# Attention and channel mix: q, k and v loaded as rows of two tokens, pair order kept through attention and mixing, and the masks of two units added by the matrix engine

## The chip, the cores and the metric

The kernel runs on one core of a Trainium2 chip. The metric is the time of one execution on the device in microseconds (us). The executions of the kernel before lay within about two per cent of each other on each chip, so each comparison uses several executions of both kernels on the same chip. An execution over 1.5 per cent above the fastest of its kernel in its round counts as slow. That is one each of four_sinks, before_bias_mix, one_sink_less_both and before_less_pe, and one or two of the kernel before in three of the five rounds. The medians and ranges quoted include them; the ratios do not, and every profiled execution is a fast one.

Names in the profile: PE is the matrix engine (PEld its weight loads), DVE the vector engine, ACT the scalar engine, POOL GpSimd, SP the engine that issues most loads and stores. A name with q behind it (SPq) is that engine's sequencer at work, for instance issuing a load.

## The reference

Attention with a sliding window of 128 tokens and four sink tokens that every query may see, then a channel mix (two layers with a squared relu between them, and a sigmoid gate), in fp32:

```python
B, H, S, D = 4, 8, 768, 64
keep = (pos_k < 4) | ((pos_q - pos_k >= 0) & (pos_q - pos_k < 128))
a = softmax(where(keep, q @ k.T / 8, -1e9)); x = (a @ v) as [B, S, 512]
x_prev = x shifted by one token, zeros first
xk = mu_k * x + (1 - mu_k) * x_prev      # mu_k, mu_r: one factor per channel
xr = mu_r * x + (1 - mu_r) * x_prev
out = sigmoid(xr @ w_r) * (relu(xk @ w_k) ** 2 @ w_v)     # w_k 512x1024, w_v 1024x512
```

## The kernel before

The work is cut into 12 units of 256 tokens, three to each of the four sequences. The order of instructions on each engine is a fixed list, made beforehand and written in the kernel, and a small model of the engines decides how the lists are interleaved and where filler matmuls go. The parts that the change and the argument touch (cuts marked):

```python
# k of units 0 to 3, q of units 0 to 7: one 512-byte row of two tokens per packet;
# v, and the other k and q: one token, 256 bytes
nc.sync.dma_start(out=buf[key][:, h0:h1, :, :]..., in_=src[b, h0:h1, ...].rearrange(
    "h (p j) d -> p h (j d)", j=2))
nc.sync.dma_start(out=buf[key][:, g, :, :],                  # v, g = 0, 1
    in_=v[b, :, s0:s0 + 128, :].rearrange("h p d -> p h d"))
...
# the values of the four sink tokens, spread over partitions by a matmul with 0/1 weights
nc.tensor.matmul(out=buf[psk]..., lhsT=spread, rhs=buf["vb", u][:, 0, :, 0:D], ...)
nc.vector.tensor_tensor(out=vsink[b % 2][:, :, 0:D], in0=buf[psk]..., in1=hmask..., op=ALU.mult)
...
# masks: after the exponential, on the vector engine, in every unit
nc.vector.tensor_tensor(out=at, in0=at, in1=m, op=ALU.mult)
...
# mix: one operation per 128 channels, t0 - 1 is the token before
nc.vector.scalar_tensor_tensor(out=buf[key][:, c0 + i, :], in0=buf[tk][:, i, :],
    scalar=mu[w][:, c0 + i:c0 + i + 1], in1=xt[:, c0 + i, t0 - 1:t0 + 255],
    op0=ALU.mult, op1=ALU.add)
```

Loads are issued by SP in the order of its list. In the built program they take turns on eight semaphores, and a load waits for the one eight places earlier to have landed before it is issued.

The softmax here doesn't subtract the row's maximum and nothing guards it: scores larger than these inputs give would overflow.

Of the kernel before, what the change touches and what calls it, by code (L numbers as in the profile page):

```python
# [16 lines left out]

CHOICE = {
    78: "ACT", 81: "ACT", 82: "ACT", 84: "ACT", 86: "ACT", 88: "DVE", 93: "DVE", 94: "DVE", 96:
    "DVE", 100: "DVE", 101: "DVE", 127: "DVE", 133: "DVE", 135: "DVE", 136: "DVE", 139: "ACT",  # L20
    140: "DVE", 149: "DVE", 190: "DVE", 191: "ACT", 192: "ACT", 217: "DVE", 264: "DVE", 272:
    "DVE", 277: "DVE", 304: "DVE", 342: "DVE", 345: "DVE", 347: "DVE", 351: "ACT", 353: "DVE",
    360: "DVE", 422: "DVE", 428: "ACT", 429: "ACT", 498: "DVE", 500: "DVE", 503: "DVE", 506:
    "DVE", 507: "ACT", 519: "DVE", 585: "ACT", 586: "ACT", 653: "DVE", 657: "DVE", 659: "DVE",
    662: "DVE", 671: "DVE", 735: "DVE", 737: "ACT", 738: "DVE", 743: "DVE", 750: "DVE", 814:
    "DVE", 815: "ACT", 824: "DVE", 884: "DVE", 886: "DVE", 890: "ACT", 891: "ACT", 1002: "DVE",
# [5 lines left out]
XD = ()  # L32
# [16 lines left out]
        89, 92, 105, 95, 98, 103, 116, 108, 113, 131, 137, 141, 128, 124, 119, 155, 134, 157,  # L49
        148, 183, 189, 168, 235, 207, 208, 211, 212, 219, 220, 160, 165, 171, 176, 215, 193,  # L50
        180, 200, 216, 186, 237, 290, 298, 291, 294, 299, 302, 248, 303, 225, 295, 240, 245,
        306, 223, 227, 276, 231, 228, 251, 260, 232, 266, 256, 310, 263, 283, 269, 311, 318,
        343, 308, 314, 329, 315, 348, 366, 374, 367, 375, 321, 370, 394, 326, 371, 332, 337,
        396, 274, 352, 378, 359, 379, 382, 407, 384, 386, 421, 387, 444, 452, 445, 453, 399,
        426, 404, 474, 410, 415, 390, 430, 391, 456, 437, 457, 448, 472, 485, 449, 462, 525,
        529, 526, 530, 499, 537, 460, 504, 538, 468, 509, 469, 553, 477, 482, 533, 493, 488,
        534, 511, 564, 556, 464, 578, 465, 541, 518, 543, 561, 549, 583, 572, 550, 587, 545,
        567, 631, 601, 546, 602, 605, 613, 606, 594, 629, 642, 614, 619, 609, 617, 610, 639,
        634, 677, 681, 678, 682, 663, 645, 689, 705, 707, 685, 650, 686, 690, 625, 670, 718,
        710, 621, 626, 693, 622, 760, 756, 764, 757, 761, 765, 721, 695, 740, 726, 715, 774,  # L60
        784, 701, 749, 768, 742, 769, 795, 702, 787, 792, 697, 772, 698, 816, 776, 780, 777,
        781, 834, 830, 838, 831, 835, 798, 839, 858, 860, 842, 803, 846, 843, 823, 854, 848,
        868, 863, 871, 855, 906, 914, 907, 850, 915, 851, 879, 874, 910, 892, 911, 918, 899,
        919, 934, 936, 922, 924, 930, 947, 931, 972, 939, 973, 980, 944, 981, 950, 976, 958,
        977, 955, 984, 926, 965, 985, 927, 990, 988, 1000, 1008, 1004, 1001, 1012, 1005, 1013,
        1009, 992, 1020, 996, 993, 997, 1016, 1018, 1021, 1028, 1024, 1029, 1025,
    ),
    "DVE": (
        70, 71, 88, 93, 94, 100, 96, 107, 101, 112, 109, 114, 110, 136, 104, 115, 118, 127, 123,
        143, 125, 120, 133, 121, 126, 135, 149, 144, 150, 151, 145, 152, 190, 146, 159, 147,  # L70
        164, 79, 80, 153, 69, 170, 140, 175, 161, 162, 166, 172, 167, 177, 173, 178, 154, 195,
        196, 202, 197, 204, 203, 210, 217, 198, 222, 205, 206, 83, 239, 244, 304, 199, 85, 241,
        305, 242, 246, 214, 247, 255, 218, 87, 277, 250, 293, 297, 278, 229, 252, 301, 253, 233,
        257, 258, 279, 264, 342, 285, 347, 280, 281, 286, 288, 345, 320, 287, 312, 325, 316,
        272, 336, 289, 322, 331, 323, 327, 282, 328, 333, 338, 334, 339, 369, 353, 275, 373,
        354, 360, 357, 361, 381, 355, 377, 363, 356, 362, 422, 388, 398, 403, 409, 400, 414,
        405, 401, 365, 411, 416, 406, 417, 412, 358, 364, 447, 432, 392, 433, 439, 434, 441,
        440, 455, 459, 498, 481, 476, 503, 451, 528, 500, 487, 506, 435, 492, 510, 436, 470,
        478, 479, 483, 443, 484, 494, 555, 495, 489, 540, 490, 442, 536, 557, 571, 513, 558,
        560, 532, 466, 514, 519, 562, 520, 563, 516, 566, 573, 521, 574, 515, 522, 589, 551,  # L80
        568, 590, 569, 517, 524, 547, 523, 653, 633, 592, 638, 596, 659, 598, 657, 591, 597,
        604, 644, 635, 640, 636, 641, 649, 599, 616, 600, 612, 665, 646, 593, 608, 647, 651,
        709, 652, 668, 662, 666, 692, 667, 711, 671, 672, 674, 673, 675, 712, 627, 680, 623,
        669, 735, 720, 714, 725, 722, 723, 676, 684, 727, 728, 688, 759, 716, 741, 717, 763,
        791, 786, 750, 767, 738, 743, 788, 789, 793, 744, 703, 794, 745, 771, 751, 747, 802,
        746, 753, 752, 754, 699, 818, 778, 782, 797, 819, 748, 821, 833, 799, 755, 800, 837,
        804, 805, 814, 862, 841, 867, 824, 825, 820, 845, 826, 864, 827, 865, 869, 884, 856,
        822, 878, 886, 870, 828, 873, 852, 875, 880, 881, 876, 909, 829, 917, 894, 897, 913,
        901, 895, 921, 902, 938, 903, 943, 896, 932, 949, 940, 941, 945, 946, 951, 954, 952,
        904, 956, 957, 898, 960, 961, 905, 967, 975, 962, 969, 968, 928, 979, 963, 971, 987,  # L90
        983, 1002, 964, 1003, 1007, 970, 1011, 1015, 994, 998, 1022, 1030, 1026,
    ),
    "ACT": (
        91, 90, 97, 111, 106, 99, 68, 67, 117, 130, 122, 132, 142, 138, 129, 182, 188, 163, 158,
        184, 78, 156, 174, 169, 81, 139, 209, 221, 236, 213, 179, 185, 194, 201, 181, 191, 187,
        243, 238, 292, 82, 300, 192, 254, 226, 249, 84, 296, 307, 86, 224, 259, 265, 261, 262,
        268, 267, 284, 270, 340, 324, 319, 344, 309, 335, 330, 349, 368, 376, 395, 372, 418,
        402, 397, 380, 420, 383, 423, 408, 385, 413, 351, 425, 446, 454, 427, 480, 475, 431,
        496, 438, 428, 501, 458, 450, 473, 486, 463, 527, 531, 429, 491, 461, 505, 539, 559,
        554, 507, 577, 535, 512, 570, 575, 579, 580, 582, 542, 544, 565, 584, 585, 588, 637,  # L100
        632, 603, 586, 655, 595, 607, 615, 630, 620, 643, 618, 611, 648, 679, 683, 664, 706,
        708, 713, 687, 691, 731, 729, 719, 733, 694, 724, 737, 758, 766, 762, 696, 775, 790,
        785, 770, 808, 796, 806, 801, 773, 812, 810, 817, 832, 836, 840, 859, 861, 866, 844,
        847, 815, 882, 849, 877, 872, 888, 908, 916, 893, 912, 900, 935, 920, 937, 942, 890,
        923, 891, 925, 948, 974, 953, 982, 959, 966, 986, 978, 991, 989, 1006, 1014, 1010, 1019,
        1017,
    ),
    "POOL": (
        73, 72, 74, 75, 76, 102, 77, 273, 271, 350, 508, 661, 739,
    ),  # L110
    "SP": (
        0, 1, 2, 3, 4, 5, 7, 6, 16, 8, 9, 10, 11, 15, 17, 12, 18, 13, 14, 19, 20, 25, 23, 24,
        21, 234, 22, 341, 346, 28, 30, 29, 313, 26, 27, 419, 424, 31, 230, 33, 34, 35, 32, 497,
        36, 317, 502, 37, 40, 38, 389, 39, 45, 393, 41, 576, 581, 42, 467, 43, 44, 46, 47, 654,
        656, 660, 658, 548, 48, 51, 49, 50, 471, 53, 52, 732, 730, 734, 736, 54, 628, 57, 58,
        55, 552, 56, 624, 809, 807, 704, 813, 811, 59, 60, 61, 779, 63, 64, 62, 700, 883, 885,
        889, 887, 65, 857, 66, 853, 933, 929, 783, 995, 999, 1023, 1031, 1027,
    ),
}


class Plan:







# [151 lines left out]
def kernel(  # L281
# [19 lines left out]
    NS = 4  # L301
# [15 lines left out]
    pool("bank", 8 - 2 * TOGETHER, [128, 512], FP32, psum)  # L317
    for name in ("ks", "qs", "vs"):
        pool(name, 3, [128, 2, H, D] if name == "vs" else [128, H, 2, D], FP32)
    pool("w32", 3, [128, NC, 512], FP32)  # L320
    pool("kb", 3, [128, 2, H, D], BF16)
    pool("qb", 3, [128, 2, H, D], BF16)
    pool("kt", 4, [128, NP, 2, 128], BF16)
    pool("qt", 4, [128, NP, 2, 128], BF16)
    pool("e", 5, [128, 2, 512], BF16)
    pool("es", 3, [128, 256], BF16)
    pool("rec", 6, [128, 2, 2, 1], FP32)
    pool("x", 3, [128, 2, Dm], BF16)
    pool("td", 3, [128, 2, 256], BF16)
# [630 lines left out]
```

## Time and profile before

The time before is 172.48 us, the median of 3 runs (171.81 to 172.6).

| what | before |
|---|---|
| span of the profiled execution | 169.6 us |
| PE / DVE / ACT busy | 94% / 90% / 76% |
| first matmul with wk / with wv | 21.75 us / 39.30 us |
| last matmul starts | 166.15 us |
| PE's gaps after 40 us | 3.0 us |
| v of unit 3 is issued | 40.8 us |

The first two rows are on the page; the rest is read from single instructions in the trace. For "PE's gaps" I take the starts of consecutive matmuls and subtract what a matmul of its size costs when PE is full; what is over by more than 60 ns is summed. A stretch at half clock counts as gaps too. The lines of the profile itself are in the prediction.

### The profile page before, as it was taken

What the parts mean: (1) busy time and instruction counts of PE and PEld (TensorE: products, weight loads), DVE (VectorE), ACT (ScalarE), POOL (GpSimd) and SP (SyncE); (2) the same over time, 40 slices, a digit from 0 to 9 for tenths busy, and PEclk for the clock granted to TensorE, in tenths of its full rate; (3) what the DMA queues carried; (4) which work ended last, traced back from release to release, by engine and by line L of the source; (5) the groups of instructions that cost most, each with busy time, mean ns of one, the idle gap of its engine ahead of it and who ended that gap; (6) DMA issues with size and microseconds to landing.
All of it is one profiled execution on the core that took longest, in us unless ns stands there. A gap on an engine that the chain in (4) does not pass through costs nothing.

```text
span 169.6 us, 4184 instructions
## 1 busy us (share of the span) xinstructions
PE 160.0 (94%) x1602; PEld 105.7 (62%) x1602; DVE 153.4 (90%) x403; ACT 129.0 (76%) x208; POOL 13.5 (8%) x31
## 2 busy tenths in 40 slices
PE   7977879799999999999999999999999999999992
PEld 2544658664657667767567786756476775877551
DVE  6288898999999999999999999999999999799542
ACT  3588797999898999897979986866829849953320
POOL 6330000000200010050000200030000000000000
PEclk9995699999999999999999999999999999999999
DMA  5999989999938979999579489969969858103033
GB/s 142 238 275 320 344 192 326 356 335 276 191 86 214 254 172 231 184 263 287 135 183 221 97 207 225 181 168 233 252 147 266 195 109 233 62 4 124 2 124 124
DMA packets 82803, 33.82 MB, mean 199 GB/s; under 512 B 64736, under 2 KB 77280, under 8 KB 82784
## 3 DMA queue, kind: packets, MB, share of 16 engines
q1 hardware_dynamic: 81728, 33.56, 80.0%
q8 instruction: 12, 0.20, 0.5%
q10 hardware_dynamic: 1056, 0.00, 0.4%
q14 instruction: 7, 0.06, 0.1%
HBM read 24.12 MB, written 6.29 MB: 179 GB/s over the span
## 4 chain that ended last, share of the span: by engine, by line
PE 82%; DVE 10%; DMA 3%; SPq 1%; issue 1%; ACT 0%; POOL 0%; DVEq 0%
PE bank L888 24%; PE bank L839 23%; PE bank L870 12%; PE bank L713 7%; PE sc L654 6%; DMA vs<-in_v_dram 3%; PE bank L752 3%; PE bank L569 2%; PE bank L701 2%; DVE e L690 2%; DVE xk L789 2%; SPq L387 1%; DVE x L729 1%; PE bank L631 1%; PE bank L809 1%
## 5 line engine op out<-in xcount | busy, mean ns | idle before, releaser
L839 PE MATMUL bank<-xk,wk_sb 128*128 128x256 bf16 x384 | 50.5, 273 | 1.1 <-DVE wk_sb L513 0.9
L676 ACT ACTIVATE e<-sc 128x1024 bf16<-128x1024 f32 (+1 forms) x48 | 44.6, 966 | 4.4 <-PE sc L654 4.4
L888 PE MATMUL bank<-wv_h,kk 128*128 128x512 bf16 x184 | 45.8, 379 | 0.0
L839 PEld LDWEIGHTS <-wk_sb 128*128 128x128 bf16 x384 | 35.3, 98 | 9.3 <-DVE wk_sb L513 1.4
L849 ACT ACTIVATE rl<-bank 128x512 bf16<-128x512 f32 x45 | 26.2, 607 | 10.3 <-PE bank L839 7.8
L690 DVE TENSOR_TENSOR e<-e,mask 128x1024 bf16<-128x1024 bf16 (+1 forms) x48 | 30.1, 639 | 0.4 <-POOL ksink L608 0.3
L888 PEld LDWEIGHTS <-kk 128*128 128x128 bf16 x184 | 16.7, 98 | 15.7 <-issue 0.5
L870 PE MATMUL bank<-wr_sb,xr 128*128 128x512 bf16 x96 | 24.2, 379 | 0.0
L789 DVE SCALAR_TENSOR_TENSOR xk<-td,mu,xt 128x256 bf16<-128x256 bf16 x48 | 22.4, 493 | 0.1
L789 DVE SCALAR_TENSOR_TENSOR xr<-td,mu,xt 128x256 bf16<-128x256 bf16 x48 | 22.5, 477 | 0.0
L876 ACT ACTIVATE th<-bank 128x512 f32<-128x512 f32 x24 | 14.8, 620 | 7.8 <-PE bank L870 7.7
L729 DVE TENSOR_TENSOR x<-bank,rec 128x256 bf16<-128x256 f32 x48 | 19.4, 416 | 0.6 <-DVE rec L726 0.3
L897 DVE SCALAR_TENSOR_TENSOR ob<-th,bank 128x512 f32<-128x512 f32 x23 | 15.6, 681 | 4.7 <-ACT th L876 2.6
L861 DVE TENSOR_TENSOR kk<-rl 128x512 bf16<-128x512 bf16 x48 | 19.4, 416 | 0.1
L713 PE MATMUL bank<-vb,e 128*128 128x65 bf16 x352 | 19.2, 195 | 0.2
L713 PEld LDWEIGHTS <-e 128*128 128x128 bf16 x352 | 16.7, 99 | 3.1 <-issue 0.6
L654 PE MATMUL sc<-qt,kt 64*128 64x128 bf16 (+1 forms) x256 | 14.8, 247 | 1.1 <-ACT kt L577 0.7
L870 PEld LDWEIGHTS <-xr 128*128 128x128 bf16 x96 | 8.9, 98 | 8.6 <-issue 0.3
L654 PEld LDWEIGHTS <-kt 64*128 64x128 bf16 x256 | 9.5, 97 | 7.3 <-issue 4.0
L761 ACT COPY xt<-bank 128x512 bf16<-128x512 bf16 x15 | 8.8, 587 | 5.3 <-PE bank L752 4.5
L701 PE MATMUL bank<-vsink,es 128*128 128x130 bf16 x64 | 12.4, 220 | 0.3 <-ACT rl L849 0.3
L779 DVE TENSOR_TENSOR td<-xt 128x512 bf16<-128x512 bf16 x24 | 10.5, 440 | 0.1
(63 smaller groups left out, 163.9 us busy)
## 6 DMA issues: line engine op xcount, KB each, us to landing
vs<-in_v_dram SPq DMA_DIRECT2D x24, 256.0 KB, 4.6
out_dram<-ob SPq DMA_DIRECT2D x23, 256.0 KB, 3.3
ks<-in_k_dram SPq DMA_DIRECT2D x18, 256.0 KB, 4.8
qs<-in_q_dram SPq DMA_DIRECT2D x7, 512.0 KB, 7.3
qs<-in_q_dram SPq DMA_DIRECT2D x10, 256.0 KB, 5.3
w<-in_moe_w_k_dram SPq DMA_DIRECT2D x2, 1024.0 KB, 10.3
w<-in_moe_w_v_dram SPq DMA_DIRECT2D x2, 1024.0 KB, 10.0
ks<-in_k_dram SPq DMA_DIRECT2D x3, 512.0 KB, 8.2
```

What stands on the lines that cost most here:

```text
L654: nc.tensor.matmul(out=sc[:, a, o0:o1], lhsT=lhs[rows], rhs=rhs[rows], start=True, stop=True)
L676: nc.scalar.activation(out=buf[ek][:, :, lo:], in_=buf[sck][:, :, lo:], func=AF.Exp, scale=scale)
L690: nc.vector.tensor_tensor(out=at, in0=at, in1=m, op=ALU.mult)
L701: nc.tensor.matmul(out=o[:, g, :, :], lhsT=buf["es", u][:, 128 * g:128 * g + 128], rhs=vsink[b % 2][:, 2 * c:2 * c + 2, :], start=True, st ...
L713: nc.tensor.matmul(out=o[:, g, a, :], lhsT=e[:, a, e0:e0 + 128], rhs=rhs, start=(T == 0 and i == 0), stop=(i == len(blocks) - 1), skip_gro ...
L729: P.op("DVE", dve(256), lambda ok=ok, rk=rk, c=c: nc.vector.tensor_tensor(out=buf["x", u][:, :, 128 * c:128 * c + 128].rearrange("p g (a d ...
L789: nc.vector.scalar_tensor_tensor(out=buf[key][:, c0 + i, :], in0=buf[tk][:, i, :], scalar=mu[w][:, c0 + i:c0 + i + 1], in1=xt[:, c0 + i, t ...
L839: nc.tensor.matmul(out=ps[:, i, :], lhsT=wk_sb[:, c, 128 * f:128 * f + 128], rhs=xk[:, c, :], start=(c == 0), stop=(c == NC - 1), skip_gro ...
L849: nc.scalar.activation(out=buf[rk], in_=buf[psk].rearrange("p (i t) -> p i t", i=2), func=AF.Relu)
L861: P.op("DVE", dve(512, 0.52), lambda f2=f2, rk=rk: nc.vector.tensor_tensor(out=buf["kk", u][:, 2 * f2:2 * f2 + 2, :], in0=buf[rk], in1=buf ...
L870: nc.tensor.matmul(out=buf[psk], lhsT=buf["xr", u][:, c, 128 * g:128 * g + 128], rhs=wr_sb[:, c, :], start=(c == 0), stop=(c == NC - 1))
L888: nc.tensor.matmul(out=buf[psk], rhs=wv_h[:, f, :], lhsT=buf["kk", u][:, f, 128 * g:128 * g + 128], start=(f == 0), stop=(f == NF - 1))
```

## The change

Its intent: fewer and larger packets in the load of v; no de-interleaving of q and k any more, because scores, values and mixing all work in pair order; less work for DVE in the opening, where PE waits for attention; and a mix that uses cheaper DVE operations. The core of the diff, cut:

```diff
+BIAS = (0, 1)                                    # units masked by the matrix engine
-  in_=v[b, :, s0:s0 + 128, :].rearrange("h p d -> p h d")      # two loads per unit
+  all of q, k, v: "h (p j) d -> p h (j d)", j=2    # one load per unit (units 0 to 2: two)
...
+# values of the half unit behind, moved to the other 64 partitions (16 copies)
+copy(out=buf[vj][64 - 64 * g:128 - 64 * g]..., in_=buf["vb", w][64 * g:64 * g + 64]...)
...
-  nc.tensor.matmul(out=buf[psk]..., lhsT=spread, rhs=buf["vb", u][:, 0, :, 0:D], ...)
+  def sink_rows():                               # once for each of four sequences
+      for h in range(H):
+          at = 32 * (h // 2) + 4 * (h % 2)
+          nc.sync.dma_start(out=vs32[b % 2][at:at + NS, :], in_=v[b, h, 0:NS, :])
...
+  nc.tensor.matmul(out=buf["sc", u, c][:, a, :], lhsT=ident, start=True,     # u in BIAS
+                   rhs=bias[T].to_broadcast([128, 2, 2, 128]), stop=False, ...)
...
-  nc.vector.scalar_tensor_tensor(...)            # 96 times
+  nc.vector.tensor_scalar(out=buf[key][:, c0 + i, :], in0=buf[tk][:, i, :],  # 96 times
+      scalar1=mu[w][:, c0 + i:c0 + i + 1], scalar2=None, op0=ALU.mult)
+  nc.vector.tensor_tensor(out=at, in0=at, in1=behind(c0), op=ALU.add)        # 48 times
-P.fill_until = 22000.0
+P.fill_until = 32000.0
```

The lists of order were made anew for all engines. Among other things the loads of wk now come later in the queue.

## The prediction

> **What bounds the kernel now.** I read the page first: busy shares, slices, chain. Then the windows of busy time, to find when the matrix engine becomes full, then the chain of waits in order of time, for what one matmul costs when it is full, and last the DMA issues with their landings.
>
> ```profile
> span 169.6 us, 4184 instructions
> PE 160.0 (94%) x1602; PEld 105.7 (62%) x1602; DVE 153.4 (90%) x403; ACT 129.0 (76%) x208; POOL 13.5 (8%) x31
> PE   7977879799999999999999999999999999999992
> PEclk9995699999999999999999999999999999999999
> DMA  5999989999938979999579489969969858103033
> PE 82%; DVE 10%; DMA 3%; SPq 1%; issue 1%; ACT 0%; POOL 0%; DVEq 0%
> ```
> ```profile
> 15.00:20.00 5.00, 4.64 (x53) 3.28 (x52) 3.73 (x12) 3.92 (x7) 0.00 (x0) 0.50 1.05 378
> 20.00:25.00 5.00, 3.24 (x29) 2.16 (x26) 5.00 (x12) 5.00 (x8) 0.00 (x0) 0.98 0.89 199
> ...
> 35.00:40.00 5.00, 5.00 (x44) 2.97 (x43) 5.00 (x14) 5.00 (x9) 0.00 (x0) 1.00 1.16 310
> 40.00:50.00 10.00, 10.00 (x97) 5.63 (x96) 9.96 (x26) 9.38 (x17) 1.25 (x3) 1.00 0.85 180
> ...
> 120.00:140.00 20.00, 20.00 (x201) 13.69 (x200) 19.80 (x52) 13.66 (x23) 0.00 (x0) 1.00 0.85 190
> ```
> ```profile
> 40.55 1.73 PE bank L888 x8
> ...
> 57.75 0.55 PE sc L654 x12
> ...
> 90.46 1.75 PE bank L839 x16
> ```
> In the slices the matrix engine (PE) is full from the ninth slice (about 34 us) to the end, and the chain, 82% PE, stays on it. Before that it has holes, and near 15 to 20 us runs at half clock. The windows (columns: stretch, length, busy PE, weight load, DVE, ACT, POOL, clock, DMA share, GB/s) say that from 20 us DVE and ACT are full too, and DMA is saturated until 40 us. The chain gives the price of a full PE: 109 ns for a 256-column matmul, 216 ns for 512, and 0.55 us for a pair of score tiles.
>
> With these prices and the spacings of matmul starts in the trace I add up what PE must do: 384 first-layer matmuls x 0.109 = 41.9 us; 184 second-layer x 0.216 = 39.7 and 16 half ones 1.7; 96 gate x 0.216 = 20.7; score pairs 16 x 0.548 + 8 x 0.436 = 12.3; 352 value matmuls x 0.029 = 10.2; 192 transposes x 0.056 = 10.8; sink work 3.6 + 0.9; the sink-row spread 0.9. Sum 142.7 us. The span is 169.6, so 27 us are lost. The first second-layer matmul (wv) starts at 39.3 us. By the order of the program 19.3 us of that work precede it, so 20 us are lost by then (fillers, half clock, waits), and some 7 us after, 2.6 of them behind the last matmul. **So the steady part is PE-bound and nearly without holes, and only the first 39 us have anything to give.**
>
> What sets that first part? The loads:
>
> ```profile
> 9.10 3.40 SPq L405 DMA_DIRECT2D w<-in_moe_w_k_dram  x2
> 12.55 5.34 SPq L370 DMA_DIRECT2D vs<-in_v_dram  x2
> ...
> 25.07 3.40 SPq L405 DMA_DIRECT2D w<-in_moe_w_v_dram  x2
> ```
> Start, time of issuing, what. By the landings in the trace, wk arrives at 18.2 and 22.6 us, wr at 30.6, wv at 34.5 and 37.4. Casts on a full ACT and DVE follow (the ACT cast of the first half of wv ends at 39.2 us), and the first wv matmul comes at 39.3.
>
> **What the Trainium skill says.** (1) "TensorE: Matmul & The Clock Gate", section "Back-to-back issue gap": N/2.4 + 2.5 ns when warm; 109 and 216 ns above agree. (2) The same page, "Part 3: Packing small matmuls — row/col tiling": matmuls on different row groups run at once, some 4 ns apart. The trace agrees: the two 64-row score matmuls of a pair start 3 ns apart, and 128 columns cost about 55 ns for both. (3) "VectorE: DVE Perf Modes", "The perf-mode tier table": a bf16 tensor_scalar from SBUF can go four wide, a tensor_tensor two wide. The trace has the second (512 elements 416 ns, 1024 elements 681 ns); nothing in it shows the first. (4) "DMA: Bandwidth & Descriptors", "Why small descriptors are slow": about 3 cycles per packet on top of size/32, so 22 against 19 cycles per 512 B (estimate from that page). The packets in the trace differ: about 20 ns for 256 B and 29 ns for 512 B, that is 40 against 29. The measurement decides.
>
> **The change part by part.**
> *Loads as 512 B rows.* 512 KB as 2048 packets x 20.5 ns / 16 engines = 2.6 us, as 1024 x 29 / 16 = 1.9. So 0.77 us saved in each of 24 loads (12 v, 8 k, 4 q): 18 us of DMA time, but behind a full PE this is hidden. In the opening it is only v of three units: 2.3 us.
> *Order of loads.* wk now comes behind v of unit 1, and all v are ahead of wr. Also eight tiny loads of sink rows are issued in a row. In the program's order of waits each load waits for the one eight places earlier, so the last tiny one is issued only when everything large has landed: a hole in the DMA of about 2.5 us (estimate: issue to landing of the first load was 3.0 us, less its 0.9 of transfer, plus issuing). This eats the 2.3 us. I put wk at 23 and 26 us (3.5 to 5 later than now), wr at 31.7, wv at 34.7 and 37.6 (about as now).
> *Masks of units 0 and 1 on PE.* 16 matmuls x 0.216 = 3.5 us, in a stretch where PE now runs 22 fillers; 19 fillers remain. Removed from DVE: eight mask products, 4 x 0.55 + 4 x 0.68 = 4.9 us.
> *Scores and values.* All score matmuls are now 128 columns in pairs: 8 x 55 ns + 0.096 for the change of mode = 0.54 us for two tiles. Per full pair of tiles nothing changes (0.548 now), for the first units of a sequence +0.11 x 8 = +0.9. Values: 32 more x 0.029 = +0.9; T>0 scores -0.2; the spread matmul falls away, -0.9. PE sum: **+0.7 us** outside the opening's biases.
> *Mix.* 96 scalar_tensor_tensor, start to start 0.40 us, become 96 tensor_scalar plus 48 tensor_tensor (0.36). If the former are four wide they should step at about 0.14 us (estimate by the skill's table): 38.4 -> 30.7 us of DVE; two wide: 36.5.
> *Evacuations and copies.* Evacuations of transposed q, k lose their stride: 0.73 -> 0.42 us on DVE, 0.75 -> 0.59 on ACT. New: 16 half-height value copies, 9 on DVE (3 us), 7 on ACT (6.5 us). Exponentials of first units get 1024 wide instead of 768: +0.22 x 16 = +3.5 us of ACT. In all DVE -2 to -7 us, ACT about +3 us. Off PE's path this costs or gives nearly nothing after 40 us.
>
> *The opening, counted.* DVE's work up to the end of unit 1's mix falls by about 3 us, so attention of units 0 to 2 is through sooner. In the new order PE has 21.5 us of useful work ahead of its first wv matmul, against 19.3. If that matmul stays at 39.3 us, what remains is 143.4 - 21.5 = 121.9 against 142.7 - 19.3 = 123.4: **1.5 us gained**. Adding up ACT from the landing of wk (cast, exponentials, seven relu at 0.48 apart, wr cast, tanh, wv cast) puts its wv cast at 37.8 to 39.2 us, so I take 38.4 for the matmul: **0.9 us more**. Sum -2.4 us: 172.5 -> 170.1, rounded to 170.0 for the lighter DVE.
>
> **The rivals.** (a) *Dense from wk on*: if PE runs without a hole from about 24.3 us with 8 us of useful work done, the rest is 135 + 4 of small losses + 2.6 of end, so the span is 166 and the time near 168.8, over 2% faster. For it: the scheduler was made anew with PE filled to 32 us, and attention lies ahead of the first layer. Against it: that layer's results need ACT's relu, which by my count cannot begin before 28 to 29 us (now 24.7), and there are only four banks. (b) *The hole in the DMA is the story*: wk even later, ACT behind; the opening gains nothing and the +0.7 us stays, 172.5 to 174. For it: the waits in the program; against it: much attention work is placed to fill the time. (c) *The DMA saving is the gain*: 18 us of DMA time is a lot, but after 40 us no matmul group waits for a DMA in the list of waits, so I give it nothing. (d) *New waits in the steady part* (value copies ahead of the value matmuls, ACT fuller): at most 1 to 2 us, and DVE's relief works the other way.
>
> **Range and chances.** Between rival (a) with a little extra, 167.4, and rival (b), 172.4, lie about four fifths. 2% faster is below 169.0 us, one microsecond from my centre with a spread of about 1.8: 0.31. Over 2% slower needs something that I don't see: 0.04. Within 2%: 0.65.
>
> **What would show it right or wrong.** PE full from about 27 to 30 us instead of 34; the first wv matmul near 38.4 us; wk landing at 23 and 26, with a dip of the GB/s at 15 to 18 us; the bias matmuls inside the first 20 us; score pairs at 0.54 us; 256-column matmuls still at 109 ns; tensor_scalar busy about 0.22 us each (0.28 if two wide); DMA share near 0.7 after 40 us without PE noticing. I am wrong if PE shows holes after 45 us, if wv's matmul comes after 40 us, or if PE is dense from 24 us.

## The result

The changed kernel takes 179.41 us (median of 4 runs, 178.5 to 179.66), against 172.14 us (170.09 to 172.6, 4 runs) for the kernel before beside it. Ratios in this document are the mean time of one kernel's fast runs over that of the kernel before in the same rounds, so they are not quite the ratio of the medians quoted. Here the ratio is 1.0437, with a 95% interval of 1.034 to 1.053: 4.4% slower. The prediction was 170.0 us, with a range up to 172.4, and gave "over 2% slower" a chance of 0.04. It was wrong.

The page of the changed kernel, the lines that answer to those of before (busy shares; slices of PE, clock, DMA; the chain by engine):

```profile
span 177.9 us, 4631 instructions
...
PE 164.0 (92%) x1771; PEld 108.5 (61%) x1771; DVE 152.8 (86%) x457; ACT 132.7 (75%) x205; POOL 16.4 (9%) x51
...
PE   5998897999929999999999999999999999999992
...
PEclk9999999999996999999999999999999999999999
DMA  4994999994199936998999999179788002110313
...
PE 36%; DVE 24%; DMA 20%; SPq 9%; ACT 6%; issue 4%; DVEq 0%; ACTq 0%
```

A slice is 4.45 us long. PE is full from the eighth slice, but the twelfth (about 49 to 53 us) has a 2, with a lower clock right behind it. That is a hole in the part that the prediction had called nearly without holes. The DMA has two holes: in the fourth slice (13 to 18 us), and in the tenth and eleventh (40 to 49 us), the second just ahead of PE's. The chain is no longer 82% PE; loads and their issuing (DMA, SPq) make 29% of it.

The same in windows (stretch, length, busy PE, weight load, DVE, ACT, POOL, clock, DMA share, GB/s), for the changed kernel, and one line of the kernel before that was not shown yet:

```profile
15.00:20.00 5.00, 4.14 (x58) 2.60 (x59) 4.95 (x18) 4.86 (x7) 0.00 (x0) 1.00 0.62 166
40.00:50.00 10.00, 10.00 (x97) 6.04 (x94) 8.32 (x25) 9.50 (x16) 0.00 (x0) 1.00 0.33 87
50.00:60.00 10.00, 6.58 (x81) 4.44 (x76) 7.88 (x20) 5.46 (x8) 3.10 (x5) 0.83 1.12 259
```
```profile
50.00:60.00 10.00, 9.96 (x113) 6.86 (x112) 10.00 (x29) 9.17 (x15) 0.09 (x1) 1.00 0.95 210
```

Between 40 and 50 us the DMA moves 87 GB/s (before: 180), and in the ten microseconds after it PE is busy for 6.58 us instead of 9.96. What was the load queue doing? SP's issues of the changed kernel (start, time spent issuing, what, how many):

```profile
11.58 3.86 SPq L656 DMA_DIRECT2D vs<-in_v_dram  x8
...
38.28 8.77 SPq L656 DMA_DIRECT2D vs<-in_v_dram  x16
47.09 0.39 SPq L385 DMA_DIRECT2D vs<-in_v_dram  x1
```

L656 is the line of the sink rows: each of these loads brings four rows of 64 numbers, 1 KB. Eight of them are issued in the opening, 16 in one go from 38.28 us, and eight later, at 59.80. The 16 keep SP for 8.8 us, and the load behind them, at 47.09, is v of unit 3, 512 KB. Before, v of unit 3 began to be issued at 40.79:

```profile
40.79 1.61 SPq L370 DMA_DIRECT2D vs<-in_v_dram  x1
```

The chain of waits shows what followed (start, length, what):

```profile
34.87 9.22 DMA ks<-in_k_dram
...
44.10 0.25 SPq L656
44.35 0.04 issue
44.39 0.29 SPq L656
...
47.09 4.96 DMA vs<-in_v_dram
...
52.08 0.43 DVE vb L614
52.51 1.03 DVE e L738
...
53.58 1.06 PE bank L757 x16
...
55.49 1.30 PE bank L941 x4
```
```profile
PE bank L757 <- DVE e L738: 3.4, 1, 3.4
```

Read it from the top. A load of k lands at 44.1 us. Only then does the queue go on: the tiny load eight places behind it had to wait for that semaphore. From there a tiny load costs 0.29 us of issuing and 0.04 us of gap, nine in a row, 3.0 us. In single instructions, the 8.77 us of the 16 loads divide as follows. Two stops in which SP waits for a load of k to land (at 42.6 and 44.1 us) take 1.13 and 1.23 us, 2.4 in all. The other 6.4 us are the issuing itself, 1.53 of them for the first load. The plan written in the kernel had counted 0.64 us for eight such loads. Then comes v, which lands at 52.05. DVE works through its list in order: it stands at the cast of v, and the mask products that PE needs for its next values are behind that cast. The list of waits (total, times, longest) puts the whole wait of PE at 3.4 us in one piece. After the hole PE runs at half clock for a while: four matmuls of 512 columns take 1.30 us, where four cost 0.86 before.

With the hole, PE's gaps after 40 us add up to 10.1 us, against 3.0 before. The last matmul starts 8.0 us later: 7.0 us of gaps and about 1.0 us of more work on PE (worked out below).

### The profile page after: what moved, and what is told of

It reads as the page before. It is cut to its first block, busy times and chain, and to the rows that moved or that the text cites. A ratio compares the mean times of both kernels' runs of the same rounds, so it can differ in the third digit from the quotient of the medians.

```text
span 177.9 us, 4631 instructions
## 1 busy us (share of the span) xinstructions
PE 164.0 (92%) x1771; PEld 108.5 (61%) x1771; DVE 152.8 (86%) x457; ACT 132.7 (75%) x205; POOL 16.4 (9%) x51
## 4 chain that ended last, share of the span: by engine, by line
PE 36%; DVE 24%; DMA 20%; SPq 9%; ACT 6%; issue 4%; DVEq 0%; ACTq 0%
PE bank L892 12%; PE bank L941 10%; SPq L385 6%; DVE e L738 6%; DMA w<-in_moe_w_k_dram 6%; PE bank L923 5%; DMA vs<-in_v_dram 5%; DMA ks<-in_k_dram 5%; DMA out_dram<-ob 4%; DVE x L774 3%; PE bank L757 3%; DVE ob L950 2%; DVE kk L914 2%; DVE xk L833 2%; DVE td L825 2%
## 5 line engine op out<-in xcount | busy, mean ns | idle before, releaser
L730 ACT ACTIVATE e<-sc 128x1024 bf16<-128x1024 f32 x48 | 47.7, 1034 | 1.5 <-PE sc L695 1.2
L902 ACT ACTIVATE rl<-bank 128x512 bf16<-128x512 f32 x42 | 24.5, 609 | 7.4 <-PE bank L892 6.5
L738 DVE TENSOR_TENSOR e<-e,mask 128x1024 bf16<-128x1024 bf16 x40 | 28.0, 704 | 0.2 <-ACT e L730 0.2
L923 PE MATMUL bank<-wr_sb,xr 128*128 128x512 bf16 x96 | 24.2, 379 | 0.4 <-ACT rl L902 0.3
L757 PE MATMUL bank<-vb,e 128*128 128x65 bf16 x256 | 15.5, 196 | 3.8 <-DVE e L738 3.4
L695 PE MATMUL sc<-qt,kt 64*128 64x128 bf16 x384 | 14.9, 217 | 0.4 <-DVE kt L601 0.3
L695 PEld LDWEIGHTS <-kt 64*128 64x128 bf16 x384 | 10.9, 94 | 5.5 <-issue 2.1
L833 DVE TENSOR_SCALAR xr<-td,mu 128x256 bf16<-128x256 bf16 x48 | 13.2, 278 | 0.1
L833 DVE TENSOR_SCALAR xk<-td,mu 128x256 bf16<-128x256 bf16 x48 | 12.9, 280 | 0.0
L813 ACT COPY xt<-bank 128x512 bf16<-128x512 bf16 x12 | 7.1, 588 | 6.6 <-PE bank L804 6.4
L839 DVE TENSOR_TENSOR xk<-xk,xt 128x512 bf16<-128x512 bf16 x24 | 10.5, 448 | 0.0
```

The costliest lines, as they stand in the source:

```text
L695: nc.tensor.matmul(out=sc[:, a, :].rearrange("p (j g t) -> p j g t", j=2, g=2)[:, j, g], lhsT=kt[rows, c, j, at:at + 128], rhs=q2[rows, g] ...
L730: nc.scalar.activation(out=buf[ek], in_=buf[sck], func=AF.Exp, scale=scale)
L738: nc.vector.tensor_tensor(out=buf[ek], in0=buf[ek], op=ALU.mult, in1=m.unsqueeze(1).to_broadcast([128, 2, 512]))
L757: nc.tensor.matmul(out=o[:, g, a, :], lhsT=e[:, a, j, g, :], rhs=vv[:, j, 2 * c + a, :], start=(T == 0 and j == 0), stop=(j == 1), skip_gr ...
L833: nc.vector.tensor_scalar(out=buf[key][:, c0 + i, :], in0=buf[tk][:, i, :], scalar1=mu[w][:, c0 + i:c0 + i + 1], scalar2=None, op0=ALU.mult)
L902: nc.scalar.activation(out=buf[rk], in_=buf[psk].rearrange("p (i t) -> p i t", i=2), func=AF.Relu)
```

## The experiments

The theory after reading: the tiny loads, each of which takes a place in an in-order queue, make the loss. The rival: the loss is in the steady part, through more work and new waits (pair-order scores and values, the value copies), and the hole is only where it shows. Eighteen versions were run besides the two kernels. All keep the lists of order of the kernel that they start from, but for the operations named, so that a part removed does not move the rest. The number of filler matmuls can still change, because the plan sets them by its own durations. The versions ran in five rounds on four chips, each with the kernel before beside it. One-sink ran in the first round only, so runs of different rounds are compared through their ratios.

### The tiny loads

**One load instead of eight.** Fetch 16 rows of each head (rows 0 to 15 of all eight heads fill 128 partitions) in one load of 32 KB; the mask keeps the four that count (its edit, and the new places of the sink keys, are cut here). The results are correct.

```diff
-            for h in range(H):
-                at = 32 * (h // 2) + 4 * (h % 2)
-                nc.sync.dma_start(out=vs32[b % 2][at:at + NS, :], in_=v[b, h, 0:NS, :])
+            nc.sync.dma_start(out=vs32[b % 2], in_=v[b, :, 0:16, :])
```

> The changed kernel with the eight sink-row loads of each sequence made one (16 rows of every head, 128 packets), so 4 tiny loads in place of 32; same result. Theory A (the queue of loads is held up by the many tiny loads: 16 in a row end at 47.1 us and push v of the fourth unit to 47 us): the hole of 3.5 us at 50 to 53.5 us and the cold clock behind it (about 1 us) go, wk lands about 2 us sooner, and the ratio to the kernel before falls from 1.044 to between 0.98 and 1.01. Theory B (the steady part is slower by its own new work: value copies, 128-column scores, fuller ACT): the hole shrinks but the ratio stays at or above 1.03. Theory C (the opening: wk too late): ratio 1.02 to 1.03 with a full PE first after 30 us.

Measured: 174.66 us (174.22 to 175.29), ratio 1.0153 (1.008 to 1.022), span 172.9.

```profile
35.18 1.50 SPq L654 DMA_DIRECT2D vs<-in_v_dram  x2
36.74 0.45 SPq L385 DMA_DIRECT2D vs<-in_v_dram  x1
```
```profile
50.00:60.00 10.00, 9.56 (x128) 6.39 (x123) 9.31 (x29) 9.14 (x15) 1.39 (x3) 1.00 0.90 239
```

v of unit 3 is issued at 36.74 us, PE's hole is gone, and 2.8 of the 4.4 per cent with it. 1.5 per cent stay. I call this kernel "one-sink" below; it is the base of most further runs.

**Four loads instead of eight**, one per pair of heads (correct):

> The changed kernel with four sink-row loads per sequence in place of eight (8 rows each; 16 loads in all, not 32); same result. Theory A: a part of the loss comes back, the series of 16 becomes 8, about 2.7 us shorter, ratio between that of one_sink and 1.044, about 1.01 to 1.03. Theory B or C: as the changed kernel, 1.035 or more.

Measured: 177.19 us (175.18 to 178.53), ratio 1.0257 (1.016 to 1.035). Between the two: v of unit 3 is issued at 43.4 us. The bytes are the same, so it is not they that count. But a load does not have one price: each of the eight ahead of v now takes 0.61 us to issue, so that the issuing still makes 5.2 us (6.4 with sixteen). What shrinks most is the wait for a place in the queue, from 2.4 to 0.3 us.

**No sink loads in sequences 1 to 3** (wrong on purpose; the eight of the opening stay):

```diff
         def sink_rows():
+            if b > 0:
+                return
```

> The changed kernel without the 24 sink-row loads of the later three sequences (the result is wrong on purpose there); the eight of the first sequence stay. It parts the hole in the opening (12 to 17 us) from the hole at 40 to 50 us. Theory A: most of the loss lies in the later loads, ratio 0.99 to 1.01; what one_sink is faster than this one is the price of the opening's eight, which I put at 1 to 2 us. Theory C: late_none stays at 1.03 or more and one_sink alone is fast.

Measured: 174.61 us (173.99 to 174.97), ratio 1.0142 (1.008 to 1.020), the same as one-sink. So the eight tiny loads of the opening, the only ones that the prediction counted, cost nothing that can be measured: they do make the hole in the DMA that it expected (147 GB/s at 15 to 20 us here, 348 in one-sink), but the first matmul with wk came at 26.2 us in both runs. What costs are those of the later sequences.

**The tiny loads alone, in the kernel before.** 32 such loads, into a buffer that nobody reads, at the corresponding places of its queue; all else as before (correct):

```diff
+        def tiny_rows(i=i):
+            for h in range(H):
+                at = 32 * (h // 2) + 4 * (h % 2)
+                nc.sync.dma_start(out=tiny[i % 2][at:at + NS, :], in_=v[i, h, 0:NS, :])
```

> The kernel before with 32 tiny loads of the same shape into tiles that nothing reads, put at the places in its queue of loads that answer to those of the change (8 behind v of the second unit, 16 ahead of v of the fourth, 8 more ahead of the next pair of transposes); nothing else changed. Theory A: it slows down by about as much, 4 to 8 us, ratio 1.02 to 1.05, with PE holes between 45 and 60 us. Theory B or C: ratio below 1.01.

Measured: 179.48 us (178.2 to 180.27), ratio 1.0422 (1.034 to 1.050). SP's issues, and the window after them:

```profile
43.52 6.87 SPq L927 DMA_DIRECT2D tiny<-in_v_dram  x16
50.43 0.39 SPq L370 DMA_DIRECT2D vs<-in_v_dram  x1
```
```profile
50.00:60.00 10.00, 7.34 (x77) 5.04 (x78) 6.06 (x17) 5.12 (x10) 0.61 (x1) 0.83 0.82 200
```

The same picture: 16 loads, 6.9 us, v of unit 3 behind them, PE short of work, and at a lower clock (0.83 in this window, 0.92 in the 20 us after it). 32 KB of loads that nobody uses cost the kernel before 4.2%. That is as much as the change's whole loss, though not a proof that its loss is only this: this kernel's later loads stand differently.

**Another queue for the later ones.** The 24 tiny loads of sequences 1 to 3 issued by GpSimd instead of SP (correct):

```diff
-                nc.sync.dma_start(out=vs32...
+                (nc.gpsimd if b else nc.sync).dma_start(out=vs32...
```

> The changed kernel with the 24 tiny sink-row loads of sequences 1 to 3 issued by GpSimd in a queue of their own, instead of the load queue in which v of unit 3 stands behind 16 of them. Theory: what costs is the place in the in-order queue; then v of unit 3 is issued near 37 us again, the hole of 3.5 us at 50 us is gone, and the time is that of the one-sink kernel, 1.010 to 1.022 of the kernel before. Rival: the small packets or the landings themselves cost; then it stays at 1.035 to 1.045. A third way, that GpSimd's issuing of 16 loads is itself late for the sink values at 50 us, would show as a wait of DVE for them.

Measured: 176.19 us (175.08 to 176.79), ratio 1.0287 (1.022 to 1.035), between both ranges.

```profile
39.10 1.58 SPq L384 DMA_DIRECT2D vs<-in_v_dram  x1
```
```profile
50.00:60.00 10.00, 9.36 (x124) 6.26 (x121) 9.49 (x28) 8.05 (x11) 5.41 (x11) 1.00 0.86 227
```

The mechanism holds: same loads, another queue, v of unit 3 is issued at 39.1 us instead of 47.1, and PE is busy for 9.36 us of the window instead of 6.58. The size is off: it comes only half way to one-sink, and so do the four loads per sequence. The list of waits shows no wait of DVE for sink rows. What the other half is, I did not settle. The traces of these two runs cannot tell, because in both the profiled execution is the fastest of the four (175.08 and 175.18 us, spans of 173.4 and 173.5 us against one-sink's 172.9).

### What is left: 1.5 per cent

Each part of the change was then put back or taken out by itself.

**Masks of units 0 and 1 on DVE again** in one-sink (correct):

```diff
-BIAS = (0, 1)
+BIAS = ()            # the mask product stands right ahead of the reciprocal of its pair
```

> The kernel with one sink load per sequence, but the masks of units 0 and 1 multiplied by the vector engine again (16 bias matmuls taken from PE, 16 mask products put back on DVE). One_sink stood at 1.0153 of the kernel before. If the bias matmuls cost PE real time (16 x 0.216 = 3.5 us that no filler gives back), this run falls to about 0.995 to 1.005. If, as the prediction had it, they lie in a stretch where PE waits anyway and spare DVE 4.9 us in the opening, this run is slower than one_sink by 1 to 2 us, 1.02 to 1.03, and the first wr and wv matmuls come later than 36 and 40.7 us.

Measured: 181.33 us (180.93 to 183.11), ratio 1.0644 (1.055 to 1.074): 4.8 per cent more than one-sink, far more than either theory said. The loads of wv show where (first this run, then one-sink):

```profile
31.42 5.02 SPq L413 DMA_DIRECT2D w<-in_moe_w_v_dram  x2
```
```profile
25.23 4.48 SPq L403 DMA_DIRECT2D w<-in_moe_w_v_dram  x2
```

Late masks make the casts of wk late, which free the buffer that wv is loaded into, so wv is issued 6 us later. But the run has the fault that before_bias shows below: the plan put 44 fillers into PE's line instead of 19, and eleven of them stand right ahead of value matmuls, from 24.9 to 28.7 us. Ten are on the chain of waits (L970 is the filler):

```profile
25.73 3.11 PE bank L970 x10
```

So the 4.8 per cent are an upper bound, of which the fillers can be 3.8 us or 2.2 per cent. That the masks on PE are a gain here and not a cost is likely, but what they are worth was not measured.

**The old mix** in one-sink, `scalar_tensor_tensor` on the same shifted data (correct):

> The kernel with one sink load per sequence, mixing by scalar_tensor_tensor again on the same shifted data (96 of them at about 0.40 us instead of 96 tensor_scalar at 0.28 busy plus 48 shifted tensor_tensor at 0.43 to 0.45). Sum by those durations: 38.4 against 26.9 + 21.1 = 48 us busy, so DVE gets lighter by up to 10 us if the new mix is really the dearer one; if DVE's weight in 15 to 40 us or in the steady part is what keeps one_sink at 1.0153, it falls to 1.00 to 1.008. If DVE is not on the path that sets the end, it stays within 0.5 per cent of 1.015.

Measured: 177.72 us (177.69 to 178.57), ratio 1.0424 (1.035 to 1.049), the opposite of what was expected. The busy times that I had added up overlap: from start to start the old operation takes 396 ns, `tensor_scalar` 196 and the addition 338 (medians). So the old mix costs 38.0 us of DVE and the new one 35.0: the new mix is a gain of 3 us on DVE, and in this order, made for the new mix, putting the old one back costs 4.6 us of time.

**A constant factor** in place of the factor per channel (wrong on purpose):

```diff
-  scalar1=mu[w][:, c0 + i:c0 + i + 1], scalar2=None, op0=ALU.mult)
+  scalar1=0.5, scalar2=None, op0=ALU.mult)
```

> Wrong on purpose: the factor of the mix is the constant 0.5 for every channel instead of a factor per partition read from SBUF. Theory: the factor per partition, held in fp32, is what keeps the tensor_scalar at 278 ns for 256 elements (about one element per ns and partition); with a constant it goes four wide, about 0.13 to 0.2 us, and 96 of them free DVE of 8 to 14 us. Rival: the operation is as slow with a constant, 0.27 to 0.28 us. For the time: if DVE is on the path, 0.5 to 1.5 us less than one_sink (1.007 to 1.012 of the kernel before); if not, 1.013 to 1.018.

Measured: 172.54 us (172.15 to 172.65), ratio 1.0105 (1.004 to 1.017). The group of one-sink with the factor read from SBUF, and that with the constant (busy us in total, mean ns of one):

```profile
L831 DVE TENSOR_SCALAR xk<-td,mu 128x256 bf16<-128x256 bf16 x48 | 13.5, 291 | 0.0
```
```profile
L831 DVE TENSOR_SCALAR xk<-td 128x256 bf16<-128x256 bf16 x48 | 10.8, 236 | 0.0
```

From start to start the constant takes 135 ns and the factor from SBUF 196. The prediction had 0.14 for "four wide": that is what the constant gives, and the factor per partition does not. The first wv matmul comes at 39.7 us instead of 40.74, so this mis-sized operation is worth about 1 us of the opening (one profiled execution of each).

**The value copies taken out** of one-sink (wrong on purpose):

> Wrong on purpose: the one-sink kernel without the 16 half-height copies of the values (9 on DVE at 0.43 us, 7 on ACT at about 0.93), the first half of each unit reading its own values instead. Theory: what is left of the loss in the one-sink kernel (1.5 per cent, 2.6 us) is DVE and ACT being so full that PE waits for them in small holes after 40 us (3.0 us against 0.6 before); 3.9 us less on DVE and 6.5 less on ACT then bring 1 to 2 us, 1.003 to 1.010 of the kernel before. Rival: it is the late opening (first wv matmul at 40.7 instead of 39.3 us) alone; then 1.012 to 1.018 stays, as only four of the copies lie before it.

Measured: 172.94 us (172.38 to 174.19), ratio 1.0132 (1.007 to 1.020). That is not separable from one-sink's 1.0153: the copies are not it.

**wk earlier in the queue** of one-sink, ahead of v of unit 0's second half (correct):

> The one-sink kernel with the two loads of wk moved in the load queue from behind v of unit 1 and k, q of unit 2 to ahead of v of unit 0's second half and of the sink row. wk then lands some 4 us earlier. If the late landing of wk (first matmul of it at 26.2 instead of 21.75 us) is what keeps the opening from gaining, the first wv matmul comes at 39.3 us or sooner and the time is 1.000 to 1.010. If DVE's and ACT's work up to there sets the opening, values and masks of units 0 and 1 get later instead and the time is 1.015 or more.

Measured: 178.38 us (177.53 to 180.0), ratio 1.0473 (1.038 to 1.056). Worse: the first matmul with wk came at 30.05 us, not earlier. It waits for attention's results, whose data now came later: wk itself landed at 14.7 and 17.5 us. This order is worse in another way, so the run alone does not acquit wk. A comparison at hand does: in the changed kernel wk landed at 24.2 and 27.5 us and in one-sink at 21.3 and 24.1, and the first wv matmul came at 40.75 and 40.74. In one-sink's chain of waits DVE makes 22.7 of the 27.3 us from 13.7 to 41 us.

**Parts of the change in the kernel before.** The masks of units 0 and 1 on PE alone:

> One part of the change alone, on the kernel before: masks of units 0 and 1 added by the matrix engine, everything else and the order as it was. If PE has idle time there (22 fillers before 30 us) and DVE is what is full, attention of units 0 and 1 ends up to 2 us earlier, and the time is 0.99 to 1.0 of the kernel before. If the 3.5 us of bias matmuls push PE's own work, 1.005 to 1.02. In no case do I expect under 0.985, because wk still lands at 18 to 23 us and the first wv matmul waits for the cast of wv.

Measured: 175.6 us (174.48 to 175.7), ratio 1.0287 (1.021 to 1.036), outside what I expected. A fault of the experiment: the plan still counted the removed masks and put ten fillers (2.3 us) ahead of the first value matmuls. Mended:

> The kernel before with only the masks of units 0 and 1 moved to the matrix engine, mended: in the run before_bias the plan still counted the removed mask products in its model and put 27 fillers in PE's line instead of 22, ten of them (2.3 us) right ahead of the first value matmuls. Here the plan counts none for them. If those fillers made the loss of 2.9 per cent, this run comes to 0.99 to 1.005 of the kernel before. Rival: the 16 bias matmuls themselves, in a line whose order was made without them, delay the scores: then 1.015 or more stays.

Measured: 172.47 us (171.4 to 173.0), ratio 1.0108 (1.004 to 1.017). The first wv matmul came at 38.33 us instead of 39.30, a gain of 1 us that is not in the time any more, which is 1.1 per cent longer. With the new mix as well:

> The run above plus the new mix on the kernel before's token order: 96 tensor_scalar (a step of 0.19 us each, as the change measured it) and 48 tensor_tensor (0.33) in place of 96 scalar_tensor_tensor (0.385 to 0.40). That takes 37.5 - 34.1 = 3.4 us from DVE. The other way round, in the one-sink kernel, the old mix cost 4.6 us of time. If the new mix is a gain by itself, this run is 0.5 to 1.5 per cent under before_bias_less_fill, and the candidate to beat both kernels (0.98 to 0.995 of the kernel before). If DVE's relief is worth something only where DVE is the bound, as in the changed kernel, and not here, the two runs are the same within 0.4 per cent.

Measured: 173.78 us (173.42 to 176.79), ratio 1.0185 (1.012 to 1.025). That is neither of the outcomes expected, and not separable from the run before. No candidate: in this order, made for other durations, the lighter operation is no gain.

### Which engine binds

The last four runs take work away (all wrong on purpose) and ask which engine sets the end.

**The mask products of units 2 to 11 away**: 40 on DVE, 24 us, in one-sink and in the kernel before.

```diff
-  P.op("DVE", dve(width, 0.52), masked, ...
+  P.op("DVE", dve(width, 0.52), masked if u < 2 else lambda: None, ...
```

> Wrong on purpose: the one-sink kernel without the mask products of units 2 to 11 (40 on DVE, steps of 0.60 us: 24 us less of DVE's work, all but two units of it after 40 us). Theory: DVE's fullness makes PE's small holes after 40 us and sets part of the time; then 2 to 4 us fall away, 0.990 to 1.005 of the kernel before. Rival: PE's own work and the order set it; then at most 0.7 us, 1.010 or more.

> Wrong on purpose: the same done to the kernel before (40 mask products of units 2 to 11 gone). The prediction had it bound by PE after 39 us, with 0.6 us of holes that DVE or ACT make: then 0 to 1.2 us fall away, 0.993 to 1.0. If it falls by 2 us or more, the kernel before was bound by DVE as well, and the prediction's first step is wrong.

Measured: one-sink 173.21 us (172.23 to 173.57), ratio 1.0112 (1.005 to 1.017); before 170.05 us (169.37 to 171.19), ratio 0.9923 (0.986 to 0.999). Neither gains much from 24 us less of DVE's work.

**One of eight second-layer matmuls away**: 23 x 0.216 = 5.0 us of PE, all after 39 us.

```diff
                     for f in range(4 * part, 4 * part + 4):
+                        if f == 5:
+                            continue
```

> Wrong on purpose: the one-sink kernel without one of eight second-layer matmuls of each output tile (23 x 0.216 = 5.0 us less of PE's work, all after 40 us). Bound by PE: all 5 us fall away, 0.985 to 0.99 of the kernel before. Bound by DVE and the order: 2 us or less, 1.003 or more.

> Wrong on purpose: the kernel before without one second-layer matmul in eight (23 x 0.216 = 5.0 us less of PE's work after 39 us). Bound by PE alone, as the prediction said: 5 us fall away, 0.970 to 0.975. Bound by DVE as closely as by PE, although PE showed hardly a hole: 2 us or less, 0.988 to 1.0.

Measured: one-sink 173.97 us (173.19 to 174.18), ratio 1.0157 (1.010 to 1.021), no gain at all; before 169.85 us (168.0 to 171.37), ratio 0.989 (0.981 to 0.998), that is 1.9 of the 5.0 us. In the trace of one-sink the gaps of PE after 40 us grow from 5.6 to 9.4 us, in that of the kernel before from 3.0 to 6.4: most of the freed time comes back as waits, for DVE above all.

**Both away** in one-sink:

> Wrong on purpose: the one-sink kernel without the mask products of units 2 to 11 (24 us of DVE) and without one second-layer matmul in eight (5.0 us of PE). If PE and DVE bound it together, either removal alone left the other as the bound, and both together bring 4 to 5 us: 0.985 to 0.995 of the kernel before. If ACT or DMA is the bound, both together bring no more than the masks alone: 1.005 to 1.012.

Measured: 171.54 us (170.84 to 173.53), ratio 1.0064 (0.997 to 1.015), span 169.1 against one-sink's 172.9. The interval of the times is too wide to tell the two ranges apart; in the profiled execution the last matmul starts 3.8 us earlier than in one-sink, more than the masks alone (1.1 us) and the matmuls alone (0.6 us) bring. The windows from 60 to 100 us, of the kernel before, one-sink and this run in turn:

```profile
60.00:80.00 20.00, 19.92 (x236) 14.39 (x235) 19.97 (x51) 18.08 (x31) 3.29 (x3) 1.00 0.99 228
80.00:100.00 20.00, 20.00 (x217) 13.57 (x217) 20.00 (x55) 17.89 (x31) 1.17 (x1) 1.00 0.74 164
```
```profile
60.00:80.00 20.00, 19.98 (x240) 14.31 (x239) 19.63 (x59) 19.29 (x33) 1.67 (x3) 1.00 1.13 226
80.00:100.00 20.00, 19.58 (x246) 13.02 (x244) 19.79 (x60) 18.64 (x34) 0.62 (x1) 1.00 1.21 250
```
```profile
60.00:80.00 20.00, 19.42 (x257) 14.28 (x256) 15.49 (x52) 19.64 (x33) 1.23 (x3) 1.00 1.08 239
80.00:100.00 20.00, 19.91 (x239) 13.96 (x237) 17.02 (x55) 19.24 (x33) 0.67 (x1) 1.00 1.24 260
```

The third column of busy time is DVE, the fourth ACT. In the kernel before PE and DVE are both full. In one-sink ACT has gone from 18.0 to 19.0 of 20 us as well. With PE and DVE relieved, ACT is still at 19.2 to 19.6, and nearly half of PE's gaps, by the semaphore that came last, are then waits for ACT (copies, relus, tanh), with 1.3 us for a load of transposed q. All this fits a steady part that is bound by PE and DVE within a microsecond or two of each other, in the changed kernel with ACT close behind. That is a reading; in the times the runs do not separate it from an order that leaves no slack.

From this the 1.5 per cent add up, as an account and not as a test of each term: one-sink's last matmul starts 3.1 us later than before. PE has 1.05 us more work by the measured steps (24 score pairs x 0.553 against 16 x 0.548 + 8 x 0.436 us: +1.0; 32 more value matmuls x 0.029: +0.9; four spread matmuls x 0.219 fewer: -0.9). Its gaps after 40 us are 5.6 us instead of 3.0: +2.6. By 40 us it is ahead by about 0.5 us of work. The sum is 3.1. Which part of the change makes the extra gaps stays open: no single relief takes them away (masks 0.4 per cent, copies 0.2, constant factor 0.5, all near the width of the intervals). I found no correct version that beats the kernel before.

## Why the prediction was wrong

By its own steps:

- **"So the steady part is PE-bound and nearly without holes, and only the first 39 us have anything to give."** The observation was right and the conclusion wrong. Few holes on PE do not say that PE alone sets the time: taking 5.0 us of PE's work away brought 1.9. DVE was as full, 19.80 of 20 us in the window from 120 us that the prediction itself showed. (ACT, called full from 20 us on, was at 13.66 there.) And a part with nothing to give has a lot to lose: 7.0 of the 9.4 us between 170.0 and 179.4 are new gaps of PE after 40 us.
- **"Also eight tiny loads of sink rows are issued in a row."** This is the step that failed most. The wait was right, and worked out: in this in-order queue each load waits for the one eight places earlier. But the issuing of many loads got no sum of its own, and it is the larger part. And the step was applied to the eight of the opening only, where the hole in the DMA came as predicted (166 GB/s at 15 to 20 us instead of 378) and cost nothing. The change has 32, and 16 of them stand ahead of v of unit 3. The size there is 8.8 us of the queue (6.4 of issuing, 2.4 of waits), a hole of 3.4 us on PE and a stretch at half clock; taking the tiny loads away is worth 2.8 of 4.4 per cent, adding them to the kernel before costs 4.2.
- **Rival (c), "after 40 us no matmul group waits for a DMA in the list of waits, so I give it nothing".** True of the kernel before, and used to dismiss every effect of a load after 40 us, though the change rewrites that queue. The wait did not even show as a wait of PE for a DMA: it came through DVE, which stood at a cast.
- **Rival (d), new waits of 1 to 2 us in the steady part.** They are 2.6 us in one-sink, where the runs of tiny loads are gone. Close, but they stayed out of the sum.
- **The opening, -2.4 us.** It gained nothing. The work ahead of the first wv matmul was as counted, but that matmul came at 40.75 us instead of 38.4. About 1 us of that is `tensor_scalar`: taken at 0.14 us a step, it took 0.196. The sum went by ACT's work from the landing of wk on. wk landed at 24.2 and 27.5 us instead of 23 and 26, but DVE, not that landing, set the opening. So rival (b) had the opening's outcome right, and its reason, the hole in the DMA, wrong.
- **Masks on PE.** The direction was probably right; the size stays open. In the changed order they are worth at most 4.8 per cent, with the casts of weights and the load of wv hanging on them, but 25 more fillers are in that number.
- **PE's sum, +0.7 us.** It was 1.05. **Mix**: the case "two wide", 36.5 us, was near (35.0). **The clock** at 15 to 20 us rose to 1.00 in the new order, and was lost again at 53 us.
- **The range.** Its upper end, 172.4 us, was called rival (b), though rival (b) itself was put at 172.5 to 174: the range left out what the prediction had named as possible.

What it had named as a sign of being wrong, holes on PE after 45 us and wv's matmul after 40 us, came both.

## What to carry to other kernels

Count the loads, not only their bytes: in an in-order queue with a fixed number of semaphores a load of 1 KB takes a place like one of 1 MB, and it has an issuing time of its own (here 0.29 us for 1 KB, 0.39 for v of a whole unit, 512 KB), so a run of small ones belongs into one larger load, or behind the large load that work is waiting for. When a change reorders a queue, ask of every long run in it what stands behind it, everywhere in the program and not only where the change was meant to act. And a full engine is not yet the bound: before giving a relief its full worth, look which other engine is as full in the same window, or take work away from each and see.

## What the Trainium skill lacked or had wrong

- "DMA: Bandwidth & Descriptors", section "Issuing engines are not separate DMA queues", says that issuing from several engines only saves sequencer time, "which is usually small relative to the DMA itself". Here it was not small: 16 loads of 1 KB kept the issuing engine for 8.8 us, of which 6.4 were issuing (0.33 us each where nothing else held them up), and moving 24 of 32 to another engine took the ratio from 1.0437 to 1.0287.
- I found no page that puts a size on the wait for a semaphore which a load some places earlier still holds. In this case it was 2.4 of the 8.8 us: SP stood still for 1.13 and 1.23 us until two loads of k, eight places earlier, had landed.
- "VectorE: DVE Perf Modes", section "The perf-mode tier table", gives `tensor_scalar` in bf16 from SBUF as four wide and does not tell a constant factor from one per partition. With an fp32 factor per partition read from SBUF, 256 elements took 196 ns from start to start, with a constant 135 ns.
